# An attention, Fourier-mix and feed-forward kernel: the places of 1750 stage instances in program order, from a formula of offsets to a table

## The chip, the core and the metric

The kernel runs on one core of a Trainium2 chip. Its engines are TensorE (PE, matmul; its weight loads are listed as PEld), VectorE (DVE), ScalarE (ACT), GpSimd (POOL) and SyncE (SP), which here only issues DMAs. Each engine executes its own instructions in the order in which the program lists them, and waits at an instruction until what that needs is there. The metric is device time in microseconds (us) of one execution.

## The reference

Eight batches, 8 heads, 576 positions, head size 64; 4608 rows of 512 in all.

```python
out_d   = sm_attn(q_d, k_d, v_d)            # q, k, v averaged over groups of 4 positions
out_up  = np.repeat(out_d, 4, axis=2)       # "pooled" attention, 144 positions
out_loc = softmax over |i - j| < 4 of 0.125 * q k^T, times v      # "local" attention
x = (out_up + out_loc) as [8, 576, 512]
u = x + real(fft(fft(x, axis=1), axis=2))   # mix
un = (u - mean) / sqrt(var + 1e-6)
return u + relu(un @ w_ch1) @ w_ch2         # 512 -> 2048 -> 512
```

The two weights come as 64-bit floats.

## The kernel before

The work is written as small stages, each a method that issues the instructions of one step, mostly on one engine. Four classes belong to the attention stage.

- `Pooled(b)`, for each batch b, in pairs of heads h0 = 0, 2, 4, 6: `sum_v` (a load on SP and three adding loads on POOL), `scores` (PE), `maxima` (DVE), `exps` (ACT), `transpose_p` (PE), `copy_p` (ACT), `values` (PE), `result` (DVE). It needs `sums`, q and k added up over groups of 4.
- `Unit(b, m)`, five for a batch, for the local attention: `load` and `load_v` (SP), `sum_in` (DVE, makes `sums`), then `scores`, `maxima`, `exps`, `transpose_p`, `copy_p`, `values`, `result` on the same engines as above.
- `Mix(b)`, the two Fourier transforms as matmuls: `half_sum` (DVE) and `half_difference` (POOL) of the results of units, `channels` and `fold` (DVE, half of the folds POOL), `split_high` (ACT) and `split_low` (POOL), `sequence` (PE, four of them, 12 matmuls each) with `sequence_high` (ACT) and `sequence_low` (DVE), a small `sequence_z`, then `mix` (PE), `even_out` (ACT), `unfold` (DVE) and the stores.
- `Quarter(n)`, 64 of them, decodes a quarter of one of 16 weight pairs f to two 32-bit parts: `fetch` (SP), `size` (ACT), `clamp` (POOL), `join` (three DVE instructions), `high` (ACT), `low` (POOL). The first three pairs are decoded during the attention stage, the other 13 only when memory of that stage has come free (`close_a`, `close_e`, `close_d`).

`Block(n)`, nine blocks of 512 rows, is the feed-forward stage: `load` (SP and POOL), `stats` and `norm` (DVE), `turn` (PE transposes, four tiles i), `turn_high` (ACT), `turn_low` (DVE), then for each f `first` (12 matmuls), `high` (ACT), `low` (DVE), `second` (12 matmuls), at the end `finish` (DVE) and `store` (SP). Blocks 0 and 1 run f = 0 to 4 first, then block 0 runs f = 5 to 15, then block 1, then the others.

The program's order comes from one list. Each `plan` method calls `at(t, stage)` with a due time t, and at the end the stages are issued by rising t. The due times are a formula: batch b begins at 20 b plus a small offset, unit u at 4 u, and each kind of stage has one offset that serves all its instances (`AT`, single numbers with two decimals). So all batches have nearly one pattern. Only the order on each engine and queue comes out of it, no wait: waits come from the data and from buffers. There are eight PSUM banks, which `bank` gives out from two pools of four in turn; six buffers for q and k (`NUM_QKT`), three for v (`NUM_V`).

Of the kernel before, what the change touches and what calls it, by code (L numbers as in the profile page):

```python
# [24 lines left out]
PACE = 20  # L25
AT = {

    "pooled": (-1.26, -1.46, -2.33, -2.53, -2.41, -2.33, -2.18, -2.27),
    "local": (0, 0.05, 0, 0, 0, 0, 0.06, 0),
    "mix": (25.89, 25.9, 24.42, 25.07, 25.13, 25.15, 25.13, 25.42),  # L30
    "local_steps": (0, 1.6, 4, 5, 6.17, 8.25, 9.86),
    "pooled_steps": (-0.43, 1.18, 2.76, 3.93, 5.01, 7.14, 8.75),
    "qk": (-10, 1.51),
    "sums": (-3.66, 0.28),
    "sum_v": (-10.41, -9.02, -3.44, 3.04),
    "load_v": (5.42,),
    "store_pooled": (1.92,),
    "pooled_splits": (0.67, 1.6, 0.62, 0.79, 0.69, 1.28, 2.49),
    "halves": (0.22, 1.82, -0.65, 1.49),
    "splits": (0.89, 2.15, 0.3, 0.93, 0.62, 1.76, 2.52),  # L40
    "z": (1.09, 5.07, 6.35, 6.73, 7.92),
    "sequence": (8.13, 2.44, 0.85, 1.44),
    "mixed": (16.42, 1.41, 1.07, 1.26, 2.3, 4.23),
    "tail": (22, 1.18, 1.17, 1.26, 1.53, 2.62),
    "store_local": (2.48,),
    "ffn": (5.82, 1.6),
    "decode": (38.91, 6.9, 4.13, 1.26, 4.33),
    "decode_steps": (-1.51, -0.25, 0.38, 2.01, 2.74),
    "first_norms": (1.77, 1.65, 6.94, 0.87),
    "second_norms": (0.74, 1.38, 3, 1.5),  # L50
    "add": (17.46, 2.35, 4.1),
# [3 lines left out]
CHUNKS = (3, 5, 9, 16)  # L55

ROUND = 5
TILES = 4
# [7 lines left out]
def kernel(  # L66
# [13 lines left out]
    nc = tc.nc  # L80
# [143 lines left out]
    def pooled_at(b):  # L224
        return PACE * b + AT["pooled"][b]

    def pooled_end(b):
        return pooled_at(b) + 15 + AT["pooled_steps"][-1]

    def unit_at(u):  # L230
        return 4 * u + AT["local"][u // NPAIR]

    def mix_at(b):
        return PACE * b + AT["mix"][b]

    events = []

    def at(t, fn, *args):
        events.append((t, len(events), partial(fn, *args)))
# [4 lines left out]
    class Pooled:  # L244
# [97 lines left out]
        def plan(self):  # L342
            b = self.b
            stages = [self.scores, self.maxima, self.exps, self.transpose_p, self.copy_p, self.values, self.result]
            for r in range(4):
                at(pooled_at(b) + AT["sum_v"][r], self.sum_v, r)
            for i in range(H // 2):
                t, h0 = pooled_at(b) + 5 * i, 2 * i
                for d, fn in zip(AT["pooled_steps"], stages):
                    at(t + d, fn, h0)  # L350
# [738 lines left out]
```

## Time and profile before

| | |
|---|---|
| median of three runs | 1195.04 us (1194.35 to 1195.20) |
| the profiled execution, its own time | 1197.92 us |
| span of its trace | 1196.1 us |
| instructions | 20340 |
| PE busy, share of the span | 1126.6 us, 94% |
| DVE busy | 578.1 us, 48% |
| ACT busy | 362.9 us, 30% |
| POOL busy | 304.7 us, 25% |

The profile is of one execution. A share of busy time over the whole span hides the stages: attention and mix lie in the first 370 us, the decoding of weights and the first rounds of the feed-forward stage between 370 and 500 us, the rest of the feed-forward stage behind. Idle time of an engine is put down to what ended it, its releaser.

### The profile page before, as it was taken

How to read it: one execution, taken by the hardware profiler on the slowest of the kernel's cores; microseconds unless marked ns; L12 is line 12 of the kernel's file. 1: busy time of each engine (PE TensorE's matmuls, PEld its weight loads, DVE VectorE, ACT ScalarE, POOL GpSimd, SP SyncE). 2: the span in 40 equal slices, each digit the busy share in tenths (PEclk: the TensorE clock that was granted, in tenths of full speed). 3: DMA queues.
4: the chain of work that ended last, by engine and by line, in shares of the span. 5: the costliest groups of instructions: out<-in, count | busy, mean ns of one | idle time of the engine just before them, and what ended most of it. 6: DMA issues, size and time to landing. Idle time of an engine off the chain costs nothing.

```text
span 1196.1 us, 20340 instructions
## 1 busy us (share of the span) xinstructions
PE 1126.6 (94%) x8172; PEld 950.9 (79%) x8172; DVE 578.1 (48%) x1226; ACT 362.9 (30%) x1050; POOL 304.7 (25%) x411
## 2 busy tenths in 40 slices
PE   4988988989977999999999999999999999999998
PEld 4777977978866888878788888888788888888886
DVE  3798988978888988532222222222222222222111
ACT  3566756757643444211111111111111111111110
POOL 2145536425448556320300200300200300200000
PEclk7888988989988999999999999999999999999999
DMA  8577658569658444250600600600600600600000
GB/s 262 185 209 239 169 168 260 156 198 275 158 120 216 138 129 124 74 111 4 137 1 1 141 1 1 141 1 1 141 1 1 141 1 1 141 1 1 36 1 35
DMA packets 57902, 123.07 MB, mean 103 GB/s; under 512 B 7280, under 2 KB 7408, under 8 KB 57552
## 3 DMA queue, kind: packets, MB, share of 16 engines
q1 hardware_dynamic: 44288, 92.23, 24.1%
q0 software_dynamic: 13520, 29.55, 14.3%
q8 instruction: 64, 1.05, 0.4%
q14 instruction: 30, 0.25, 0.1%
HBM read 89.88 MB, written 30.74 MB: 101 GB/s over the span
## 4 chain that ended last, share of the span: by engine, by line
PE 76%; DVE 11%; DMA 9%; issue 1%; ACT 1%; POOL 1%; SPq 0%; DVEq 0%; POOLq 0%; ACTq 0%
PE hps L814 30%; PE acc L832 10%; PE acc L834 10%; PE acc L833 10%; PE y L578 4%; DMA vsum<-in_vg_dram 2%; DMA ut<-ud 2%; PE av L457 2%; DVE xs L520 2%; DVE w L531 2%; DMA qkT<-in_qk_dram 2%; PE avd L311 2%; PE tpn L785 1%; PE sc L398 1%; DVE o L641 1%
## 5 line engine op out<-in xcount | busy, mean ns | idle before, releaser
L822 DVE SCALAR_TENSOR_TENSOR hl<-hps,hh 128x512 fp32r<-128x512 f32 x144 | 99.4, 690 | 455.4 <-ACT hh L818 455.0
L814 PE MATMUL hps<-unT,w1h 128*128 128x512 f32 x1152 | 311.6, 392 | 1.8 <-ACT even L630 1.2
L814 PEld LDWEIGHTS hps<-unT,w1h 128*128 128x128 f32 x1152 | 215.2, 188 | 47.7 <-ACT even L630 1.4
L818 ACT ACTIVATE hh<-hps 128x512 fp32r<-128x512 f32 x144 | 86.1, 598 | 547.2 <-PE hps L814 547.2
L832 PE MATMUL acc<-w2h,hh 128*128 128x512 f32 x576 | 226.7, 394 | 0.0
L834 PE MATMUL acc<-w2h,hl 128*128 128x512 f32 x576 | 225.3, 391 | 0.0
L833 PE MATMUL acc<-w2l,hh 128*128 128x512 f32 x576 | 225.2, 391 | 0.0
L814 PE MATMUL hps<-unT,w1l 128*128 128x512 f32 x576 | 155.2, 391 | 0.0
L814 PEld LDWEIGHTS hps<-unT,w1l 128*128 128x128 f32 x576 | 108.2, 188 | 23.7
L834 PEld LDWEIGHTS acc<-w2h,hl 128*128 128x128 f32 x576 | 108.2, 188 | 23.6
L832 PEld LDWEIGHTS acc<-w2h,hh 128*128 128x128 f32 x576 | 108.3, 188 | 22.6
L833 PEld LDWEIGHTS acc<-w2l,hh 128*128 128x128 f32 x576 | 108.3, 188 | 22.6
L770 POOL TENSOR_TENSOR rstd<-rstd,mhalf 128x1 f32<-128x1 f32 x36 | 20.7, 575 | 307.5 <-DVE rstd L769 307.5
L755 POOL DMA_DIRECT2D ut<-ux x40 | 35.6, 1058 | 209.6 <-DMA ut<-um 207.4
L416 ACT ACTIVATE sb<-sc,mx 128x64 f32<-128x64 f32 x320 | 69.8, 329 | 1.3
L457 PE MATMUL av<-vaug,pT 64*64 64x65 f32 x1280 | 48.8, 230 | 5.9 <-DMA vaug<-in_vw_dram 5.5
L384 DVE TENSOR_REDUCE sums<-qkT 128x224 f32<-128x896 f32 (+4 forms) x48 | 43.3, 944 | 17.5 <-DMA qkT<-in_qk_dram 16.3
L457 PEld LDWEIGHTS av<-vaug,pT 64*64 64x64 f32 x1280 | 44.7, 145 | 8.4 <-issue 6.1
L398 PEld LDWEIGHTS sc<-qkT 64*64 64x64 f32 x1280 | 48.2, 147 | 3.8 <-issue 1.1
L794 DVE TENSOR_TENSOR unT<-tpn,unT 128x512 fp32r<-128x512 f32 x36 | 24.8, 688 | 53.2 <-ACT unT L791 53.2
L398 PE MATMUL sc<-qkT 64*64 64x64 f32 x1280 | 48.1, 230 | 0.0
L558 POOL TENSOR_TENSOR fl<-xeo,fh 128x512 fp32r<-128x512 f32 x32 | 44.0, 1376 | 15.1 <-ACT fh L555 14.9
(97 smaller groups left out, 1442.8 us busy)
## 6 DMA issues: line engine op xcount, KB each, us to landing
qkT<-in_qk_dram SPq DMA_DIRECT2D x40, 512.0 KB
raw<-in_wq_dram SPq DMA_DIRECT2D x64, 256.0 KB
vaug<-in_vw_dram SPq DMA_DIRECT2D x40, 260.0 KB
out_dram<-ut SPq DMA_DIRECT2D x36, 256.0 KB
um<-o SPq DMA_DIRECT2D x16, 512.0 KB
ut<-ux POOLq DMA_DIRECT2D x32, 256.0 KB, 5.5
ut<-ud POOLq DMA_DIRECT2D x32, 256.0 KB, 5.4
vsum<-in_vg_dram POOLq DMA_DIRECT2D x24, 292.5 KB, 6.4
```

Of the source, the lines that this page charges most:

```text
L384: nc.vector.tensor_reduce(out=to, in_=x[:, :, a - g0 : e - g0], axis=AX.X, op=ALU.add)
L398: nc.tensor.matmul(sc[r, a * W : (a + 1) * W], self.qkT[r, 0, a // 2, o : o + W], self.qkT[r, 1, a // 2, o : o + W], start=False, stop=Tru ...
L416: nc.scalar.activation(out=self.sb[:, a], in_=self.sc[:, a * W : (a + 1) * W], func=AF.Exp, scale=0.125, bias=self.mx[:, a : a + 1],)
L457: nc.tensor.matmul(av[r, a, :], pT[r, 4 * hh + a], va[r, 4 * hh + a, :], start=True, stop=True)
L558: nc.gpsimd.tensor_sub(out=self.fl[:, t], in0=self.x[t], in1=self.fh[:, t].bitcast(F32))
L578: nc.tensor.matmul(y, l, r, start=(i == 0), stop=(i == len(mms) - 1))
L814: nc.tensor.matmul(hps, a[:, c, :], unT[:, x, c, :], start=(i == 0), stop=(i == len(mms) - 1))
L818: nc.scalar.activation(out=hh, in_=self.hps[f], func=AF.Relu)
L822: nc.vector.scalar_tensor_tensor(out=hl, in0=self.hps[f], scalar=0.0, in1=self.hh[f].bitcast(F32), op0=ALU.max, op1=ALU.subtract)
L832: nc.tensor.matmul(acc, hh, w2h, start=start, stop=False)
L833: nc.tensor.matmul(acc, hh, w2l, start=False, stop=False)
L834: nc.tensor.matmul(acc, hl, w2h, start=False, stop=stop)
```

## The change

Every stage instance up to a certain point of the program gets its own place, a whole number from 0 to 1749, in a table with one row for each kind of stage (`TURNS`). `at` takes the next number of the row of its stage; an instance for which the row has run out (the feed-forward stage from block 1, f = 9, on) keeps a due time by the old formula and comes behind all places. All 2502 stage instances are there before and after, and each issues the same instructions. Two small edits go along: `sums`, `yh`, `o` and `ends` are allocated by whichever of their stages comes first, since that is no longer always the same one.

```diff
-PACE = 20
-AT = {
...
-    "pooled_steps": (-0.43, 1.18, 2.76, 3.93, 5.01, 7.14, 8.75),
-    "qk": (-10, 1.51),
-    "sums": (-3.66, 0.28),
-    "load_v": (5.42,),
-    "local_steps": (0, 1.6, 4, 5, 6.17, 8.25, 9.86),
-    "halves": (0.22, 1.82, -0.65, 1.49),
-    "sequence": (8.13, 2.44, 0.85, 1.44),
-    "first_norms": (1.77, 1.65, 6.94, 0.87),
...
+ITEM = 1.6
+TURNS = {
...
+    "Unit.load": (
+        0, 2, 1, 6, 8, 44, 43, 42, 72, 73, 104, 154, 153, 150, 157, 155, 288, 294, 292, 357, 361, 358, 402, 405,
+        476, 530, 528, 657, 656, 658, 751, 752, 814, 820, 816, 879, 881, 947, 946, 981,
+    ),
...
+    "Unit.load_v": (
+        9, 5, 4, 45, 102, 106, 152, 149, 158, 232, 230, 289, 355, 362, 360, 406, 471, 472, 475, 529, 560, 653,
+        655, 698, 695, 753, 818, 817, 822, 880, 943, 945, 944, 984, 1032, 1098, 1099, 1097, 1163, 1161,
+    ),
...
+    "Unit.scores": (
+        17, 16, 34, 38, 40, 57, 108, 122, 111, 146, 220, 251, 282, 256, 341, 320, 387, 386, 469, 500, 524, 591,
+        601, 623, 707, 708, 720, 759, 760, 857, 810, 908, 926, 968, 973, 1013, 1061, 1109, 1087, 1111,
+    ),
...
+    "Unit.maxima": (
+        20, 22, 49, 60, 61, 87, 115, 138, 139, 203, 239, 265, 301, 295, 391, 334, 436, 443, 488, 538, 558, 607,
+        633, 681, 714, 716, 766, 778, 779, 865, 853, 934, 940, 977, 980, 1042, 1072, 1120, 1107, 1132,
+    ),
...
+    "Mix.sequence_low": (
+        229, 217, 238, 243, 376, 407, 414, 411, 557, 556, 559, 573, 711, 733, 693, 712, 892, 897, 891, 893,
+        1023, 1041, 1022, 1058, 1175, 1201, 1176, 1192, 1296, 1297, 1275, 1273,
+    ),
...
+    "Block.stats": (1159, 1154, 1178, 1157, 1323, 1295, 1324, 1351, 1747),
...
+    "Block.norm": (1202, 1203, 1231, 1217, 1331, 1303, 1379, 1380),
...
+    "Block.turn": (1208, 1209, 1232, 1219, 1335, 1375, 1407, 1406),
...
+    "Block.turn_low": (1216, 1233, 1260, 1276, 1349, 1402, 1416, 1421),
...
+    places = {name: iter(turns) for name, turns in TURNS.items()}
     events = []
...
-    def at(t, fn, *args):
-        events.append((t, len(events), partial(fn, *args)))
+    def at(fn, *args, t=0.0):
+        owner = getattr(fn, "__self__", None)
+        name = fn.__name__ if owner is None else f"{type(owner).__name__}.{fn.__name__}"
+        place = next(places.get(name, iter(())), None)
+        events.append((place is None, t if place is None else place, len(events), partial(fn, *args)))
...
-            t = unit_at(self.u)
-            for fn, (first, step) in ((self.load, AT["qk"]), (self.sum_in, AT["sums"])):
-                at(pooled_at(self.b) + first + step * self.m, fn)
-            at(t + AT["load_v"][0], self.load_v)
-            stages = [self.scores, self.maxima, self.exps, self.transpose_p, self.copy_p, self.values, self.result]
-            for d, fn in zip(AT["local_steps"], stages):
-                at(t + d, fn)
+            for fn in (
+                *(self.load, self.sum_in, self.load_v, self.scores, self.maxima, self.exps),
+                *(self.transpose_p, self.copy_p, self.values, self.result),
+            ):
+                at(fn)
...
-        for _, _n, fn in sorted(events, key=lambda e: e[:2]):
+        for *_, fn in sorted(events, key=lambda e: e[:3]):
```

Sorting the stages by the formula and by the table gives the order on each engine. Of the 2502 instances 756 keep their place in the whole list; the first that moves is the first of all, the last is number 2390. Some stretches of the two orders (P is Pooled, U is Unit; arguments are batch and unit or head):

```
PE, its first 15 stages
formula: P.scores(0,0) U.scores(0,0) P.transpose_p(0,0) P.scores(0,2) U.scores(0,1) U.transpose_p(0,0) P.values(0,0)
         P.transpose_p(0,2) U.scores(0,2) U.values(0,0) P.scores(0,4) U.transpose_p(0,1) P.values(0,2) U.scores(0,3) ...
table:   U.scores(0,1) U.scores(0,0) P.scores(0,0) P.scores(0,2) U.transpose_p(0,0) P.transpose_p(0,0) U.values(0,0)
         U.scores(0,2) P.scores(0,4) U.transpose_p(0,1) P.transpose_p(0,2) U.scores(0,3) P.scores(0,6) U.scores(0,4) P.values(0,0)
SP, its first loads
formula: P.sum_v(0,0) U.load(0,0) (0,1) (0,2) (0,3) (0,4) U.load_v(0,0) P.sum_v(1,0) U.load(1,0) U.load_v(0,1) U.load(1,1) ...
table:   U.load(0,0) (0,2) (0,1) P.sum_v(0,0) U.load_v(0,2) (0,1) U.load(0,3) (0,4) U.load_v(0,0) U.load(1,2) (1,1) (1,0) ...
DVE, from the last result of a unit on
formula: result(7,4) channels(7,2,0) channels(7,2,1) stats(0,1) fold(7,2,0) unfold(6,1,0) half_sum(7,1) unfold(6,1,1)
         channels(7,1,0) stats(0,2) channels(7,1,1) fold(7,1,0) half_sum(7,0) stats(0,3) norm(0,0) ... turn_low(0,3)
table:   result(7,4) fold(7,3,0) half_sum(7,0) sequence_low(6,3) sequence_low(6,1) norm(0,0) ... turn_low(0,3)
PE, from the last values of a unit on
formula: values(7,4) mix(6,1,0) mix(6,1,1) turn(0,0) sequence_z(7) turn(0,1) turn(0,2) sequence(7,0) turn(0,3) first(0,0)
         sequence(7,1) first(0,1) sequence(7,2) second(0,0)
table:   values(7,4) sequence(6,3) sequence(6,1) mix(6,0,0) turn(0,0) turn(0,1) mix(6,1,1) sequence_z(7) turn(0,3) mix(6,0,1)
         turn(0,2) sequence(7,3) (7,2) (7,1) (7,0) first(0,0) first(0,1) second(0,0)
```

Counts on the two orders: PE stages between a unit's `scores` and its `transpose_p`, 8.8 on average by the formula and 13.3 by the table; DVE stages between a unit's `maxima` and its `result`, 18.4 and 22.6; DVE stages between a batch's last `fold` and its first `sequence_low`, batches 0 to 7, 10, 10, 9, 9, 7, 8, 5, 9 and 11, 7, 14, 11, 19, 13, 15, 8; PE stages between a pooled `transpose_p` and its `values`, 4.2 and 3.7; DVE stages between the last result that a `half_sum` needs and that `half_sum`, 12.9 and 6.8; the loads of q and k stand 29 places earlier in the whole list, on average. Of the 580 calls of `bank`, 9 by the formula and 125 by the table come at a point of the list at which all four banks of the pool that is due are held by stages whose last reader is listed later.

## Rows read from the trace of the kernel before

**Rows 1.** The head of the page: the span; PE's busy time in 40 slices of 30 us, in tenths; DVE's.

```profile
span 1196.1 us, 20340 instructions
...
PE   4988988989977999999999999999999999999998
...
DVE  3798988978888988532222222222222222222111
```

**Rows 2.** Busy time by stretch (windows): stretch and its length, busy us (instructions) of PE, PEld, DVE, ACT and POOL, granted clock, mean busy share of the DMA engines, GB/s.

```profile
0.00:20.00 20.00, 9.05 (x102) 7.91 (x104) 7.46 (x12) 3.69 (x11) 4.70 (x14) 0.74 0.85 254
20.00:50.00 30.00, 23.30 (x386) 20.13 (x384) 17.50 (x45) 17.93 (x71) 5.39 (x10) 0.81 0.80 250
50.00:100.00 50.00, 45.08 (x693) 40.04 (x690) 41.80 (x101) 31.97 (x116) 19.68 (x25) 0.91 0.60 167
100.00:150.00 50.00, 45.47 (x673) 40.62 (x671) 46.66 (x108) 33.57 (x118) 27.29 (x31) 0.90 0.72 219
150.00:200.00 50.00, 43.64 (x587) 39.45 (x587) 41.08 (x96) 28.16 (x99) 21.04 (x27) 0.86 0.66 192
200.00:250.00 50.00, 46.40 (x695) 41.84 (x696) 47.39 (x119) 35.38 (x124) 26.34 (x34) 0.97 0.74 225
250.00:300.00 50.00, 42.87 (x652) 38.83 (x650) 38.45 (x92) 31.49 (x112) 18.38 (x23) 0.93 0.75 218
300.00:350.00 50.00, 47.84 (x703) 44.42 (x704) 40.40 (x106) 31.01 (x109) 20.10 (x27) 0.97 0.58 138
350.00:400.00 50.00, 34.12 (x188) 29.56 (x187) 45.29 (x92) 18.28 (x44) 37.36 (x47) 0.83 0.73 180
400.00:450.00 50.00, 48.85 (x223) 39.98 (x222) 45.65 (x92) 22.08 (x54) 27.30 (x45) 1.00 0.47 132
450.00:500.00 50.00, 50.00 (x222) 41.46 (x221) 39.83 (x74) 20.40 (x50) 27.80 (x43) 1.00 0.35 100
...
600.00:700.00 100.00, 100.00 (x449) 82.32 (x448) 24.30 (x44) 12.90 (x22) 9.23 (x12) 1.00 0.19 42
```

**Rows 3.** The waits of PE over the whole span: engine, line that waited, releaser, total us, times, longest.

```profile
PE tpn L785 <- DVE un L777: 16.5, 4, 14.8
...
PE sp L266 <- DVE sums L384: 11.6, 2, 9.9
...
PE avd L311 <- DMA vsum<-in_vg_dram: 4.9, 1, 4.9
...
PE mix L623 <- DVE o L641: 3.9, 1, 3.9
```

**Rows 4.** The waits of DVE between 15 and 370 us, same columns.

```profile
DVE yl L588 <- ACT yh L585: 11.8, 9, 3.3
...
DVE mx L411 <- PE sc L398: 8.7, 9, 2.5
...
DVE sums L384 <- DMA qkT<-in_qk_dram: 8.0, 3, 4.0
...
DVE rsd L322 <- PE avd L311: 7.9, 3, 7.2
```

**Rows 5.** From the timeline of the first 62 us, three engines' queues (start, length, engine, line, operation, tiles, count, idle before): first PE's, then SP's loads of q and k for batch 1, then the DVE that sums them up.

```profile
15.09 1.24 PE L266 MATMUL sp<-sums 64*72 64x144 f32 x8 [9.94 <-DVE sums L384]
...
26.78 2.15 PE L311 MATMUL avd<-vsum,ptd 72*72 72x65 f32 x16 [4.88 <-DMA vsum<-in_vg_dram]
...
18.57 13.94 SPq L366 DMA_DIRECT2D qkT<-in_qk_dram  x3
...
41.33 4.11 DVE L384 TENSOR_REDUCE sums<-qkT 128x224 f32<-128x896 f32 x5
```

**Rows 6.** The transposes of block 0 and its first matmuls, from the timeline between 345 and 375 us, same columns.

```profile
365.44 1.09 PE L785 MATMUL tpn<-ident,un 128*128 128x128 f32 x4 [14.79 <-DVE un L777]
...
373.46 1.20 PE L814 MATMUL hps<-unT,w1h 128*128 128x512 f32 x4 [0.67 <-ACT unT L791]
```

**Rows 7.** A piece of the chain that ended last, between 380 and 390 us: start, us, what; one `sequence` and one `first`.

```profile
385.34 1.60 PE y L578 x12
...
386.94 2.82 PE hps L814 x12
```

**Rows 8.** VectorE between 352 and 366 us, from the timeline: the last instructions of `result(7,4)`, two `half_sum` (L520) and the first `norm` (L777).

```profile
353.43 0.75 DVE L475 TENSOR_TENSOR xb<-av,rs 128x256 f32<-128x256 f32 x2
...
357.18 3.31 DVE L520 TENSOR_TENSOR xs<-xa,xb 128x512 f32<-128x512 f32 x1
...
363.14 0.69 DVE L520 TENSOR_TENSOR xs<-xa,xb 128x512 f32<-128x512 f32 x1
...
364.75 0.54 DVE L777 TENSOR_SCALAR un<-ut,mv,rstd 128x512 f32<-128x512 f32 x1
```

**Rows 9.** Groups of instructions by line and form: engine, operation, tiles, shapes, count, busy us, mean ns, idle before. `half_sum`, then `channels` of the sums and of the differences.

```profile
L520 DVE TENSOR_TENSOR xs<-xa,xb 128x512 f32<-128x512 f32 x24 | 26.0, 1082 | 0.0
...
L531 DVE TENSOR_TENSOR w<-xs 128x255 f32<-128x255 f32 x24 | 17.4, 727 | 0.1
...
L531 DVE TENSOR_TENSOR w<-xm 128x255 f32<-128x255 f32 x24 | 10.4, 433 | 0.0
```

**Rows 10.** The last weight of a `first`: GpSimd's low part of pair 15, and that pair's first use on PE, from the timeline between 484 and 505 us.

```profile
492.16 0.74 POOL L191 TENSOR_TENSOR w1l<-wt,w1h 128x256 fp32r<-128x256 f32 x1 [1.76 <-ACT w1h L187]
...
493.71 1.07 PE L814 MATMUL hps<-unT,w1h 128*128 128x512 f32 x4
```

More of the change, by code (lines that the diff above doesn't have):

```diff
@@ L372, in sum_in @@
         def sum_in(self):
-            if self.m == 0:
+            if self.b not in sums:
                 sums[self.b] = pd.tile([P, 2, HP, G], F32, name="sums", bufs=1)
@@ L649, in store_mixed @@
             k0 = TAIL * (self.b % 2)
-            for half, o in enumerate(self.o):
+            for half in range(2):
                 dst = um[self.b][half, k0 : k0 + 2 * P, :].rearrange("(t k) c -> k t c", t=2)
-                nc.sync.dma_start(out=dst, in_=self.o[o])
+                nc.sync.dma_start(out=dst, in_=self.o[half])
         def store_ends(self):
@@ L675, in plan @@
         def plan(self):
-            t = mix_at(self.b)
-            local = list(reversed(range(NSL)))
-            first, step, first_m, step_m = AT["halves"]
-            for i, slot in enumerate(local):
-                at(t + first + step * i, self.half_sum, slot)
-                at(t + first_m + step_m * i, self.half_difference, slot)
-            for begin, name, these in ((pooled_end(self.b), "pooled_splits", [NSL]), (t, "splits", local)):
-                first, step, odd, minus, plus, high, low = AT[name]
-                for i, slot in enumerate(these):
-                    u = begin + first + step * i
-                    at(u, self.channels, slot, 0)
-                    at(u + odd, self.channels, slot, 1)
-                    at(u + minus, self.fold, slot, 1)
-                    at(u + plus, self.fold, slot, 0)
-                    at(u + high, self.split_high, slot)
-                    at(u + low, self.split_low, slot)
@@ L721, in plan @@
-            at(unit_at(NPAIR * self.b + NPAIR - 1) + AT["local_steps"][-1] + AT["store_local"][0], self.store_local)
+            for slot in reversed(range(NSL)):
+                at(self.half_sum, slot)
+                at(self.half_difference, slot)
+            for slot in reversed(range(NSL + 1)):
+                for odd in range(2):
+                    at(self.channels, slot, odd)
+                for minus in range(2):
+                    at(self.fold, slot, minus)
+                at(self.split_high, slot)
+                at(self.split_low, slot)
@@ new lines, in plan @@
+            for pooled in (True, False):
+                at(self.split_z, pooled)
+            for fn in (self.sequence_z, self.z_high, self.z_low):
+                at(fn)
+            for T in range(4):
+                for fn in (self.sequence, self.sequence_high, self.sequence_low):
+                    at(fn, T)
+            for slot in range(2 + self.b % 2):
+                at(self.mix, slot, 0)
+                at(self.even_out, slot)
+                at(self.mix, slot, 1)
+                for minus in range(2):
+                    at(self.unfold, slot, minus)
@@ L867 @@
         u.plan()
[L868 to L880 removed]
+    at(constants)
+    at(clear_yz)
     def close_b():
```

308 lines of the change are left out of this document (187 added, 121 removed), and 32 rows, old and new, of the table TURNS.

## The prediction

> **What bounds the kernel now.** I read the head of the page first, then busy time by stretch, then the waits of PE and of DVE, then the timelines of the start and of the handover to the feed-forward stage. The slices [rows 1] show three regimes. From some 500 us on PE is at 9 tenths or more and DVE at 2 or 3: PE does 100 of 100 us at full clock [rows 2], and no order of stages can shorten that. Between 40 and 500 us DVE is as full as PE. From 50 to 350 us the six rows of DVE add up to 255.8 of 300 us and those of PE to 271.3, so DVE stands 44.2 us and PE 28.7 us [rows 2]. Before 50 us both are short of data: DVE does 25.0 of 50 us, PE 32.4 [rows 2]. From 350 to 400 us DVE does 45.3 of 50 us and PE only 34.1 [rows 2], most of which is one wait of 14.8 us for the first `norm` [rows 3, 6].
>
> So the end is set like this: a fixed piece of full PE work behind 500 us, and before it a stage in which DVE is nearly the limit, PE waits for DVE at some places and DVE for PE or a load at others. All that a new order can do is to take out idle time before 500 us: of PE some 63 us (the rows to 500 us add up to 436.6 us of PE) and of clock. Where the granted clock of a row is under 1 [rows 2], its PE time is longer by about that share: 0.26 of 9, 0.19 of 23, 0.09 of 45, 0.10 of 45, 0.14 of 44, 0.03 of 46, 0.07 of 43, 0.03 of 48, 0.17 of 34, together some 33 us, an estimate.
>
> **The change, part by part.** It removes and adds no operation; every term is idle time, so each is bounded by the idle time of its stretch. I took the two orders apart by engine; the counts are those given with the change.
>
> *The start, to 50 us.* By the formula PE's first stage is `scores` of the pooled attention, which needs the sums of five loads and starts at 15.1 us after a wait of 9.9 us; the seventh stage then waits 4.9 us for the sum of v [rows 3, 5]. By the table two `scores` of units come first, which need one load each, and the pooled `values` that waited is the fifteenth stage: the eight stages that now stand before it cover 4.9 us with about 1 us each, if v comes no later. Against that, two of the five loads are issued behind a load of the sum of v (292.5 KB) and two of v (260 KB), 0.81 MB or 3.2 us at 254 GB/s [rows 2], so the pooled stages begin up to 3 us later. Batch 1's loads stand 13.9 us in SP's queue until `scores` of units free their buffers, and DVE sums them only at 41.3 us [rows 5]; the table has those `scores` earlier. Between nothing (the loads run at 0.80 and more of the DMA engines all the while [rows 2]) and -10 us (9.9, or 4.9 and as much for batch 1) I take -5, the wait of 4.9 us that has an evident cover.
>
> *50 to 350 us.* DVE's named waits up to 370 us are 11.8 us of `sequence_low` for PE and ScalarE, 8.7 of `maxima` for `scores`, 8.0 of the sums for loads, 7.9 of a pooled `result`, 7.2 of these at once in the start [rows 4]. The table pulls producers forward and pushes consumers back: between the last `fold` and the first `sequence_low` of a batch lie 12 DVE stages on average instead of 8, between a unit's `scores` and its `transpose_p` 13.3 PE stages instead of 8.8, and the loads of q and k stand 29 places earlier in the list. What waits is then covered by work of the same engine. If all of 11.8, 8.7 and 8.0 went, it would be -28; but PE and DVE are both over 85% full here, and with one wait gone the next comes soon after. Pooled `values` follow their `transpose_p` closer than before (3.7 stages for 4.2, and in one case none), which costs PE some waits for ScalarE, free as long as DVE is the later one. Ends 0 and -28; I take half, -14.
>
> *The handover.* After the last `result` of a unit DVE has 13 stages before the first `norm`, from 354.2 us to 364.8 us, 10.6 us of which one `half_sum` takes 3.3 [rows 8]; by the table four stages. Three of the `stats` and other work of the thirteen now stand ahead of that `result`, so not all of 10.6 us is won. PE gets two `sequence` (1.6 us each [rows 7]) into the gap that was empty. Against it, all four `sequence` of batch 7, 6.4 us, now stand before the first `first`, which was behind one of them; this is work that had to be done anyway, not a loss, but the last `turn_low` is also three stages later in DVE's order. Ends 0 and -14.8 (the gap [rows 6]); I take half, -7.
>
> *The clock.* 33 us of PE time are due to the lower level, and it falls where PE has stood: 0.83 in the stretch with the gap of 14.8 us against 1.00 behind it [rows 2, 6]. A third less idle time should give some of it back: 0 to -8, taken -3.
>
> *The first rounds of the feed-forward stage.* In four cases (f = 0 and 15 of block 0, f = 1 of block 1, f = 7 of block 0) only one `first` of 2.8 us [rows 7] stands between `first` and its own `second`, where there were two stages. One ScalarE and one VectorE instruction must fit under it, behind whatever DVE has queued (45.7 of 50 us busy [rows 2]). Never shown before; bounds nothing and +5 (one wait of PE for DVE is 3.9 us [rows 3], for one case of four and a little for the others); taken +2.
>
> Sum: -5 - 14 - 7 - 3 + 2 = -27. The profiled execution's span is 1196.1 us, its own time 1197.9, 2.9 above the median of 1195.0; the difference applies to both, so I predict 1195 - 27 = 1168 us. If every term took half of its amount, 1182; with all terms nearer to their ends, -45, 1150.
>
> **What could eat some of it.** `half_sum` took 0.69 us in one place and 3.31 in another, where a GpSimd instruction ran beside it, 1.08 on average; `channels` of the sums 0.73, of the differences 0.43 [rows 8, 9]. Undisturbed the 24 and 24 would take 16.6 and 10.4 us instead of 26.0 and 17.4, so 16.4 us of DVE go that way. By the table a `half_sum` comes 6.8 stages after the result that frees it, not 12.9, and GpSimd's `half_difference` waits for the same result: they meet more often. If the loss doubled, +16, the sum would be -11, 1184 us; this lies in the forecast's own range. The Trainium skill (SBUF — State Buffer, Who interferes with whom) states that a VectorE instruction with two SBUF inputs contends with a GpSimd instruction that reads SBUF and that the order of issue decides which of them blocks; by that rule such a meeting costs either engine, and the stretched rows agree.
>
> **The rivals.** *The banks (slower).* The table makes PE run far ahead: 125 calls for a PSUM bank against 9 come when the list still holds all four. Where this happened before, a matmul of `mix` stood 3.9 us until an `unfold` had read its bank [rows 3]. PE has 28.7 us to lose from 50 to 350 us [rows 2]; 116 more calls use that up at 0.25 us each. At 0.35 us they cost 40.6 us, 12 more than PE has, and start and handover give nothing as the whole stage is late: 1207 us. Against it: the list's place says little of time where DVE, which frees the banks, is not held up itself, and then a full set of banks only means that DVE always has work waiting.
>
> *The weights (no change).* GpSimd finishes the last weights of pair 15 at 492.9 us and PE uses them at 493.7, 0.8 us later [rows 10]. Should the decoding end when it did, any gain before it is lost again there, and the time stays within 0.2%, 1195 us. For it: DVE, which does most of the decoding, is 91% busy from 400 to 450 us [rows 2]. Against it: the decoding starts with memory that the attention stage frees, in the table's order as in the formula's after about the same DVE work, so it moves along with the handover; and from 450 to 500 us DVE has 10.2 us to spare [rows 2].
>
> **How the numbers follow.** Forecast 1168, own range 1150 to 1184, 79%; weights 1195, 7%; banks 1207, 14%. About 0.2% or 2.4 us is what a measurement of this kernel tells from no change. Faster 0.79, same 0.07, slower 0.14. The range of 8 in 10 has to take in the own range, its tail above 1184 and the weights: 1150 to 1198, which leaves out most of the banks and what lies under 1150.
>
> **What would show it.** Start: PE's first stage well before 15 us and no wait for the sum of v. Middle: DVE's six rows of 50 us fuller, the waits of `sequence_low`, `maxima` and sums under half of 28 us. Handover: the gap of 14.8 us before the first transposes under 8 us. Clock: rows nearer to 1. Feed-forward: PE without gaps of over 1 us between the first `first` and 500 us, and the last weights still just in time, but some 25 us earlier. I am wrong if PE stands for banks (releasers `unfold`, `result`, `exps` before matmuls that don't read them), if DVE's busy time before the handover grows, or if the last weights come at 493 us again.

## The result, and the profile after

The changed kernel took 1150.51 us (median of 4 runs, 1145.82 to 1151.62) against 1194.69 (4 runs): ratio 0.962, 95% interval 0.959 to 0.965, 44.2 us less. The forecast was 1168, 27 less. The direction was right and the size too small: the time lies at the low edge of the range of 1150 to 1198 (by the ratio, 0.9622 of 1195.04 us, it is 1149.9). Idle time fell where the prediction looked for it; what PE loses at its lower clock was put far too low. The profiled execution after is the fastest of its four (1145.82 us, span 1144.0) and that of before was 2.9 us above its median, so the two profiles differ by 52 us, 8 more than the medians.

The head of the page after: span, busy time of the engines, then PE's and DVE's busy slices and the granted clock, in slices of 28.6 us; it answers [rows 1].

```profile
span 1144.0 us, 20389 instructions
...
PE 1108.0 (97%) x8172; PEld 935.8 (82%) x8172; DVE 545.4 (48%) x1226; ACT 358.4 (31%) x1050; POOL 293.5 (26%) x411
...
PE   7899999899889999999999999999999999999998
...
DVE  4889999899878776322212222222222222222111
...
PEclk7999999999999999999999999999999999999999
```

PE (with its weight loads), DVE, ACT and POOL have as many instructions as before; the 49 more of the total are not theirs. PE executes the same 8172 matmuls in 1108.0 us instead of 1126.6, 18.6 us less. The record of the clock in the traces says where from: before, 60.4 us of PE's work lie in stretches at half clock, after, 20.2 us, which is 30 and 10 us more than at full clock. In slices the clock is at 9 (90% or more) in all but the first. A second profile of the same order (t_all, below) has PE at 1110.5 us, 16.1 less than before. PE's idle time, span less busy time, is 36 us instead of 69.5. Idle and clock together are the 52 us.

Busy time by stretch after, columns as in [rows 2].

```profile
0.00:20.00 20.00, 13.14 (x142) 11.18 (x144) 8.44 (x14) 5.20 (x18) 4.70 (x14) 0.68 0.87 286
20.00:50.00 30.00, 26.45 (x508) 23.42 (x505) 22.51 (x62) 21.92 (x89) 9.16 (x14) 0.93 0.87 253
50.00:100.00 50.00, 45.99 (x774) 41.31 (x774) 43.66 (x119) 36.87 (x135) 27.98 (x35) 1.00 0.86 254
100.00:150.00 50.00, 47.64 (x715) 43.18 (x714) 47.91 (x118) 36.35 (x128) 24.12 (x31) 1.00 0.73 221
150.00:200.00 50.00, 48.13 (x737) 43.53 (x735) 46.74 (x126) 35.85 (x127) 25.00 (x32) 1.00 0.81 251
200.00:250.00 50.00, 45.49 (x720) 40.92 (x719) 44.78 (x107) 33.86 (x123) 22.46 (x29) 0.97 0.73 206
250.00:300.00 50.00, 49.13 (x778) 46.10 (x779) 45.84 (x129) 37.53 (x133) 26.71 (x35) 1.00 0.78 207
300.00:350.00 50.00, 42.49 (x297) 37.04 (x296) 39.75 (x97) 20.67 (x48) 34.54 (x48) 0.97 0.73 185
350.00:400.00 50.00, 49.82 (x229) 40.44 (x228) 40.68 (x86) 21.06 (x53) 23.32 (x41) 1.00 0.41 128
400.00:450.00 50.00, 50.00 (x221) 41.21 (x220) 37.88 (x78) 20.38 (x52) 25.15 (x43) 1.00 0.34 104
```

Against [rows 2] PE does more matmuls in each row to 300 us, and four of the five rows from 50 to 300 us are at full clock, where they were at 0.86 to 0.93: from 150 to 200 us PE is busy for 48.1 us at 1.00 where it was for 43.6 at 0.86. The clock is no higher in the first 20 us (0.68 for 0.74) and from 200 to 250 us (0.97 in both). The six rows of DVE from 50 to 350 us add up to 268.7 us for 255.8. From 300 us on the rows hold other work than before, since the feed-forward stage begins earlier.

The same columns with cuts at the end of the last `result` of batch 0 and of batch 7, which bound nearly the same work in both; first the kernel before, then after.

```profile
0.00:60.45 60.45, 41.63 (x630) 35.99 (x630) 31.20 (x76) 27.70 (x102) 13.23 (x28) 0.80 0.73 223
60.45:354.19 293.74, 262.67 (x3847) 237.68 (x3847) 253.60 (x607) 186.09 (x653) 133.88 (x164) 0.92 0.68 196
354.19:1196.00 841.81, 822.33 (x3695) 677.21 (x3695) 293.28 (x545) 149.07 (x296) 157.60 (x221) 0.99 0.26 62
```

```profile
0.00:49.23 49.23, 39.59 (x644) 34.60 (x645) 30.18 (x74) 26.35 (x102) 13.08 (x27) 0.83 0.87 265
49.23:306.14 256.91, 241.89 (x3799) 219.88 (x3799) 235.43 (x616) 182.80 (x649) 131.71 (x168) 0.99 0.78 226
306.14:1144.00 837.86, 826.48 (x3731) 681.35 (x3729) 279.79 (x540) 149.24 (x301) 148.67 (x217) 1.00 0.25 62
```

Length less PE's busy time is PE's idle time: 18.8, 31.1, 19.5 before, 9.6, 15.0, 11.4 after. So 36.8 of the 52 us come out of the middle, and more than half of that (20.8) is PE's busy time, most of it clock: the middle's matmuls are nearly as many (3799 for 3847), the granted clock 0.99 for 0.92.

The waits of PE after (the longest, whole span), columns as in [rows 3], then DVE's between 10 and 340 us, as in [rows 4].

```profile
PE y L744 <- ACT fh L721: 3.8, 1, 3.8
...
PE avd L483 <- DMA vsum<-in_vg_dram: 3.2, 3, 1.2
PE tpn L932 <- DVE un L924: 2.9, 3, 1.4
PE sc L559 <- ACT sb L584: 2.4, 3, 1.7
PE sp L438 <- DVE sums L552: 2.3, 1, 2.3
...
PE mix L789 <- ACT sb L584: 1.5, 1, 1.5
```

```profile
DVE rs L639 <- PE av L625: 8.3, 15, 2.1
DVE unT L941 <- ACT unT L938: 5.8, 3, 4.3
DVE sums L552 <- DMA qkT<-in_qk_dram: 4.7, 5, 2.2
...
DVE rsd L494 <- PE avd L483: 2.2, 4, 1.0
...
DVE yl L754 <- ACT yh L751: 1.6, 2, 1.2
```

No wait of PE is over 4 us; before, there were waits of 14.8, 9.9 and 4.9. DVE's waits for `sequence_low` fell from 11.8 to 1.6 and those for the sums from 8.0 to 4.7; the wait of a unit's `result` for its `values` has grown from 1.9 us in 7 pieces to 8.3 us in 15, the mark of a VectorE that is ahead of PE.

The handover after, from PE's timeline, columns as in [rows 6], then the last low part of pair 15 on GpSimd and that pair's first weight load of this part and first matmul, as in [rows 10].

```profile
310.32 1.11 PE L932 MATMUL tpn<-ident,un 128*128 128x128 f32 x8 [1.09 <-DVE un L924]
...
321.67 1.82 PE L744 MATMUL y<-seqm,fh 128*128 128x290 f32 x6 [3.77 <-ACT fh L721]
...
329.32 1.10 PE L958 MATMUL hps<-unT,w1h 128*128 128x512 f32 x4
...
446.11 0.74 POOL L371 TENSOR_TENSOR w1l<-wt,w1h 128x256 fp32r<-128x256 f32 x1
...
446.84 1.07 PE L958 MATMUL hps<-unT,w1h 128*128 128x512 f32 x4
447.52 0.87 PEld L958 LDWEIGHTS hps<-unT,w1l 128*128 128x128 f32 x4
```

The gap of 14.8 us is one of 1.1, with 3.8 later for the last split. The first `first` comes 44 us earlier than before, and so do the weights: the last one lands at 446.85 and is loaded at 447.5.

### The profile page after: what moved, and what is told of

It reads as the page before. It is cut to its first block, busy times and chain, and to the rows that moved or that the text cites. A ratio compares the mean times of both kernels' runs of the same rounds, so it can differ in the third digit from the quotient of the medians.

```text
span 1144.0 us, 20389 instructions
## 1 busy us (share of the span) xinstructions
PE 1108.0 (97%) x8172; PEld 935.8 (82%) x8172; DVE 545.4 (48%) x1226; ACT 358.4 (31%) x1050; POOL 293.5 (26%) x411
## 4 chain that ended last, share of the span: by engine, by line
PE 79%; DVE 10%; DMA 6%; issue 2%; SPq 1%; ACT 1%; POOL 0%; DVEq 0%; ACTq 0%; POOLq 0%
PE hps L958 34%; PE acc L976 11%; PE acc L978 11%; PE acc L977 11%; DMA vsum<-in_vg_dram 3%; PE y L744 2%; PE av L625 1%; PE avd L483 1%; PE sc L566 1%; PE tpn L932 1%; DVE sums L552 1%; DMA raw<-in_wq_dram 1%; PE mix L789 1%; DVE xeo L710 1%; DVE w L697 1%
## 5 line engine op out<-in xcount | busy, mean ns | idle before, releaser
L958 PEld LDWEIGHTS hps<-unT,w1l 128*128 128x128 f32 x576 | 108.3, 188 | 23.6
L902 POOL DMA_DIRECT2D ut<-ux x40 | 35.5, 1002 | 206.7 <-DMA ut<-um 206.3
L625 PEld LDWEIGHTS av<-vaug,pT 64*64 64x64 f32 x1280 | 42.2, 138 | 6.3 <-issue 2.9
```

Of the source, the lines that this page charges most:

```text
L625: nc.tensor.matmul(av[r, a, :], pT[r, 4 * hh + a], va[r, 4 * hh + a, :], start=True, stop=True)
L902: nc.gpsimd.dma_start(out=to, in_=ux[b][k0 : k0 + m, :], accum_op=ALU.add)
L958: nc.tensor.matmul(hps, a[:, c, :], unT[:, x, c, :], start=(i == 0), stop=(i == len(mms) - 1))
```

## The experiments

b_fill and the four kernels named for an engine (b_dve, a_dve, b_pe, a_pe) add work, a_warm adds warm-up; all others issue the same instructions and change only the numbers in the table. Costs are ratios to the kernel before on the same chip, with their 95% interval, turned into us of its 1192 to 1194.

**Parts of the change in time.** A table in which the first places come from one order and the rest from the other, here one row of it:

```diff
 "Unit.scores": (          # changed kernel
-    17, 16, 34, 38, 40, 57, 108, 122, 111, 146, 220, 251, 282, 256, 341, 320, 387, 386, 469, 500,
 "Unit.scores": (          # h_start: table for 110 places, then formula
+    17, 16, 34, 38, 40, 57, 108, 137, 169, 200, 221, 254, 291, 327, 362, 384, 418, 457, 498, 529,
...
 "Mix.sequence_low": (     # h_att: table for 1100 places, then formula; its last eight
-    1023, 1041, 1022, 1058, 1175, 1201, 1176, 1192, 1296, 1297, 1275, 1273,
+    1023, 1041, 1022, 1058, 1140, 1151, 1160, 1172, 1262, 1283, 1299, 1324,
```

> The first 110 places of the list follow the table, all others the formula. Theory A (the gain is PE's idle time, taken out stretch by stretch, and with it the low clock that stood behind each of those waits): the start alone is worth what the changed kernel won there, 7.2 us of PE's idle time before 50 us, and some of the low clock at 25 and 46 us comes back, so 1183 to 1188 us against 1194.7. Rival C (the gains are one chain, the start gives nothing while DVE's order behind it is the old one, because DVE catches up later at its own pace): within 2.5 us of the kernel before, and the idle time taken out before 50 us shows again as waits between 50 and 350 us.

Measured: 0.9969 (0.9945 to 0.9993), 3.7 us less, near the prediction's 5, though under theory A's 7 to 12. The interval, 0.8 to 6.6 us, does not rule out rival C's 2.5 here.

> The first 1100 places follow the table (start and attention up to the last batch), the rest the formula, so that the handover to the feed-forward stage keeps its old order. Theory A: start (7.2), middle (15) and the greater part of the low clock (some 12 of 18.6 us of PE's busy time) are won, the handover's 9.3 us and the low clock behind it are not: 1158 to 1164 us. Rival C (the handover decides): over 1180 us, with the time won earlier lost again in the wait for the first norm, which would then be well over 14.8 us.

Measured: 1162.9 us, 0.974 (0.970 to 0.977), 31.5 less: theory A. Its handover still has the old wait:

```profile
PE tpn L1008 <- DVE un L1000: 14.8, 1, 14.8
```

> The first 1100 places follow the formula, the rest the table: the handover alone. Theory A: the gap of 14.8 us shrinks to under 5 us and the 17 us at half clock behind it go as well, some 8 us of PE's time: 1176 to 1184 us. Rival C (the handover decides): 1165 us or less. If the two halves are additive, the gain here and the gain of the kernel that has only the attention part by the table add up to 44 us within 4 us.

Measured: 0.9958 (0.9939 to 0.9977), 5.0 less, under theory A's 11 to 19 and far from rival C. PE's timeline in its handover:

```profile
353.01 1.11 PE L1008 MATMUL tpn<-ident,un 128*128 128x128 f32 x8 [1.09 <-DVE un L1000]
...
364.23 1.82 PE L820 MATMUL y<-seqm,fh 128*128 128x290 f32 x6 [3.61 <-ACT fh L797]
```

The gap is gone as in the changed kernel, 14.8 against 1.1, and 3.6 of it come back at the split; the first `first` comes at 371.95 us, only 1.5 us earlier than in [rows 6]. Theory A also counted 17 us at half clock behind the gap as 8 us of PE's time. The trace of the kernel before has only 4.1 us of PE's work in that stretch, most of which lies in the gap itself, so 2 us at most were to be had. The stretches are worth 3.7 (start), 31.5 - 3.7 = 27.8 (middle) and 5.0 alone or 12.7 (44.2 - 31.5) behind a reordered middle; the two differences are good to some 5 us. Rival C, one place that decides all, is out. The two halves add up to 36.5 of 44.2 us, not within the 4 us that were expected of additive parts: the handover seems to be worth more behind the new middle.

**The clock by itself.** The old order, and matmuls without use in seven waits of PE:

```diff
+FILL = {(1, 0): 13, (2, 6): 18, (4, 0): 13, (7, 0): 19}
...
+            two = [bank("sp", GH) for _ in range(2)]
+            fill(two[0], FILL.get((self.b, h0), 0))
...
+            fill(tp, 120 if (self.n, i) == (0, 0) else 0)
```

> The order of before, unchanged; seven of PE's waits (at 45, 60, 73, 109, 154, 258 and 365 us) are filled with matmuls without use, of the two transposes' unit matrix, into the bank that the stage behind the wait overwrites. They are 13 to 120 in number, each of some 0.1 us, about as long as the wait was. PE waits for the same data as before, but it has not stood. Theory A (the low clock is a price of its own, paid behind each wait): the low periods behind these seven waits go (6.83, 3.41, 3.41, 10.24, 6.83, 6.83 and 17.07 us, 54.6 us at half clock, up to 27 us of PE's time); where DVE is not late anyway this shows in the time: 8 to 15 us faster than before, 1180 to 1187 us. Rival B (the low clock only goes along, DVE sets the time there): the granted clock is 1 and the time stays within 2.5 us of before, or is some us longer where the filling outlasts the wait.

Measured: 1.0038 (1.0018 to 1.0058), 4.5 us *longer*. The filling of the handover's wait and its stretch, in the timeline and in the windows:

```profile
353.19 13.28 PE L247 MATMUL tpn<-ident 128*128 128x256 bf16 x120
368.07 0.66 PE L796 MATMUL tpn<-ident,un 128*128 128x128 f32 x4 [1.60 <-DVE un L787]
```

```profile
350.00:400.00 50.00, 46.38 (x335) 39.88 (x335) 45.41 (x89) 17.83 (x42) 38.15 (x48) 1.00 0.77 188
```

The filling ends 1.6 us before the first `norm` is there, and the clock of the stretch is 1.00 where it was 0.83 [rows 2]. From this transpose to the first matmul of `first` with pair 15 the trace has 128.1 us, before 128.3 [rows 6, 10]: a full clock behind the greatest wait was worth 0.2 us. But little was at stake there: the 17 us at half clock hold 4.1 us of PE's work, 2 us more than at full clock. Over the whole span PE is busy for 1147.9 us, of which the 249 matmuls without use take 33.8 (by lines), so PE's own work took some 1114 us instead of 1126.6, 12 us faster, and none of it shows in the time. In five of the other six places the next stage begins as soon as the filling ends, so that there it may have outlasted the wait; that part of the 4.5 us is not separated. The mean granted clock is 0.979 for 0.964, not 1 as rival B had it. So theory A's 8 to 15 us are refuted for this filling, and rival B is the nearer one; that the low clock costs the old order nothing is not shown.

**Which engine sets the pace.** The same extra work in both orders:

```diff
             nc.vector.tensor_reduce(out=mx, in_=scv, axis=AX.X, op=ALU.max, negate=True)
+            nc.vector.tensor_reduce(out=mx, in_=scv, axis=AX.X, op=ALU.max, negate=True)
```
```diff
+            for _ in range(7):
+                nc.tensor.matmul(sc[:, : 2 * P], one[:, :P], one, start=True, stop=True)
```

> The order of before. The maxima of each unit are computed twice into the same tile: 40 VectorE instructions more, by the 0.68 us of the one that is there, 27 us. Filling PE's waits has shown that the low clock behind them is worth nothing by itself in this order. Theory D (before the handover VectorE sets the pace of the old order, PE's waits and its clock only go along): 18 to 27 us longer than before. Rival P (PE sets the pace in both orders): at most 8 us. Rival L (neither; a chain of waits that changes between them): 9 to 17 us.

> The order of the table, with the same 40 VectorE instructions more (27 us). Against the changed kernel's 1150.5 us: Theory D (the table has filled VectorE's idle time and PE has become the pace): at most 14 us, less than the same work costs in the old order. Rival P: at most 8 us, as in the old order. Rival L: 9 to 17 us, as in the old order. Should it cost the full 27 us, VectorE is still the bound in the new order.

> The order of before, with seven matmuls without use (each some 0.1 us) ahead of each unit's scores, into the bank that these overwrite: 280 more, 30 us of PE's time at full clock. Theory D (VectorE sets the pace of the old order): at most 10 us longer than before. Rival P (PE does): 25 us or more. Rival L: 11 to 20 us.

> The order of the table, with the same 280 matmuls more (30 us). Against the changed kernel's 1150.5 us: Theory D (PE has become the pace): 20 us or more, and clearly more than in the old order. Rival P: 25 us or more, as in the old order. Rival L: 11 to 20 us, as in the old order.

| extra work | in the old order | in the table's order, less the changed kernel's 0.9622 |
|---|---|---|
| VectorE, 27 us | 1.0081 (1.0049 to 1.0114): 9.7 us | 0.9723 (0.9694 to 0.9752): 12 us |
| PE, 30 us | 1.0058 (1.0033 to 1.0083): 6.9 us | 0.9770 (0.9736 to 0.9803): 17.7 us |

(Less 0.9634, the table's order measured again below, the last column is 10.6 and 16.2 us.) No theory holds whole. VectorE is not the pace of the old order: two thirds of 27 us vanish in idle time, as theory L has it. But the 280 matmuls cost more than twice as much in the new order as in the old, as theory D has it, though not in full. Part of that is the clock. PE's busy time is 1126.6 us in the old order and 1108.0 in the new without these matmuls; with them the pages of b_pe and then of a_pe have:

```profile
PE 1144.2 (95%) x8452; PEld 962.6 (80%) x8452; DVE 577.5 (48%) x1226; ACT 362.7 (30%) x1050; POOL 303.5 (25%) x411
```

```profile
PE 1139.1 (98%) x8452; PEld 957.6 (82%) x8452; DVE 544.8 (47%) x1226; ACT 358.0 (31%) x1050; POOL 291.4 (25%) x411
```

These are 17.6 and 31.1 us more. In the old order the added matmuls also filled waits, and PE's work at half clock fell from 60 to 28 us; in the new order there was little of it to take back (20 to 15 us). Per us of PE's busy time the cost is 0.4 in the old order and 0.6 in the new, so the difference between the orders is smaller than the table makes it look. In the old order no single engine is the limit; the time goes in waits of one for the other.

**Loads or computing stages.**

```diff
 "Unit.load": (     # f_loads: formula's order, loads moved forward
-    1, 3, 4, 5, 6, 38, 47, 51, 58, 65, 133, 147, 160, 170, 183, 284, 302, 315, 328, 340,
+    0, 2, 1, 6, 8, 44, 43, 42, 68, 73, 104, 150, 154, 153, 172, 200, 288, 292, 296, 354,
...
 "Unit.load": (     # t_loads: table's order, loads where the formula has them
-    0, 2, 1, 6, 8, 44, 43, 42, 72, 73, 104, 154, 153, 150, 157, 155, 288, 294, 292, 357,
+    1, 3, 4, 5, 6, 38, 47, 51, 58, 65, 133, 147, 160, 170, 183, 284, 302, 315, 328, 340,
```

> All stages that compute keep the formula's order; only the loads on SP and POOL move forward, to about the places that the table gives them: those of q and k by 23 places of the list on average (the table: 29; six buffers and the formula's order of the units allow no more), those of v by 16 and the sums of v by 9. Theory W (what the table wins in the middle is mostly data that is there in time): 15 us or more faster than before. Rival O (it is the order of the computing stages, which leaves each engine something to do while another works): within 5 us of before.

> The reverse: all stages that compute follow the table, the loads stand where the formula has them among those stages (29, 16 and 9 places later than the table's). Against the changed kernel's 1150.5 us: Theory W: 15 us or more longer, with waits of VectorE for the tiles of q and k and of PE for v. Rival O: at most 6 us longer.

Measured: f_loads 1.0304 (1.0281 to 1.0327), 36 us *longer*; t_loads 0.9649 (0.9626 to 0.9671), 1151.0 us, the gain nearly whole. Rival O. The waits of SP's queue to 400 us and of PE from 50 to 300 us in f_loads:

```profile
SPq L610 <- PE sc L642: 108.3, 14, 15.7
```

```profile
PE av L701 <- DMA vaug<-in_vw_dram: 8.9, 1, 8.9
PE avd L559 <- DMA vsum<-in_vg_dram: 7.1, 1, 7.1
```

A load that is issued early stands in its queue until a buffer is free (108 us in all for `scores`, before 23.6), and the loads of v behind it can stand with it: the two waits of PE for v above are 16 us. What the rest of the 36 us is was not separated. By t_loads the 29 places by which the table has the loads earlier are no part of the gain: without them the time is 0.9649, with them 0.9634 (t_all below), within the intervals.

**The table again, and a warm start.**

```diff
-WARM_UP = 40
+WARM_UP = 80
```

> The order of the table for all 2502 instances, written as places throughout: the same order on every engine as in the changed kernel, to be compared with the others of this call on one chip. Both theories: 0.962 of the time of before, 1147 to 1152 us.

> The changed kernel with 80 matmuls of the warm-up ahead of its first stage in place of 40, so that PE does not stand from 4.8 to 8.3 us, right before its clock falls to half for 17 us; 13.8 us of PE's work lie in these 17 us, 6.9 us more than at full clock. Theory D (in the new order PE sets the pace, so the clock counts): 3 to 7 us faster than the same order with 40. Rival (at the start the loads set the pace, PE's clock counts for nothing there): within 2 us of it, with the same work done by 50 us.

Measured: t_all 0.9634 (0.9606 to 0.9662), 1149.5 us; a_warm 0.9668 (0.9634 to 0.9701), 1154.9, not faster. The start of a_warm, PE's timeline:

```profile
9.63 1.10 PE L566 MATMUL sc<-qkT 64*64 64x64 f32 x32
15.10 2.20 PE L438 MATMUL sp<-sums 64*72 64x144 f32 x16 [4.37 <-DVE sums L552]
```

The first two `scores` of units run at full clock, and PE then waits 4.4 us for the sums instead of 2.3: the loads set this place, the clock has nothing to give. The rival's "same work done by 50 us" does not hold in this profile: PE has done 104 matmuls fewer by then, warm-up apart, behind a wait of 5.0 us for the sum of v (3.2 in t_all, 1.2 in the changed kernel's profile).

**Classes of stages, and mean shifts.** Each stage wanted its place of one order or the other, or a mean; pairs that stand the same way round in both orders kept it.

```diff
 "Mix.sequence_low": (
-    197, 212, 224, 244, 359, 374, 387, 409, 516, 535, 547, 562, 681, 697, 708, 727, 846, 862,   # formula
+    225, 216, 233, 245, 370, 396, 402, 399, 551, 549, 552, 566, 703, 725, 699, 716, 885, 890,   # x_mix
+    214, 212, 226, 240, 377, 393, 398, 412, 535, 548, 555, 571, 691, 706, 707, 725, 862, 890,   # x_nomix
+    219, 221, 227, 240, 375, 397, 398, 405, 549, 556, 558, 567, 704, 724, 709, 726, 876, 887,   # t_mean
```

> The stages of the Fourier mix follow the table, all others the formula, as far as pairs of stages that stand the same way round in both orders allow: on VectorE 580 of the 1283 pairs that the table turns round are turned, on PE 185 of 655. Theory M (the win comes from the mix: half sums right behind the result that frees them, sequence_low later behind its sequence): 25 us or more faster than before. Rival S (the parts don't add, each stage needs the others' new places around it): within 8 us of before.

> The complement: the attention, load, decoding and feed-forward stages follow the table, the mix follows the formula, within the same bounds: 641 of the 1283 pairs on VectorE are turned, 428 of 655 on PE. Theory M: within 10 us of before. A rival that has the attention stages carry the gain (scores further ahead of their transposes, maxima further ahead of the results): 25 us or more faster. Rival S: within 8 us of before, and the sum of this gain and that of the kernel with only the mix by the table is far under 44.

> Every attention and mix stage stands at its place by the formula plus the mean shift that the table gives its kind (and its number within the batch) over the eight batches, kept to pairs that stand the same way round in both orders; the rest as in the table. So all batches have the new leads and nearly one pattern again: on VectorE 759 of 1283 pairs are turned, on PE 378 of 655. Theory K (the leads of the kinds are the gain, a formula with other offsets would have done): 30 us or more faster than before. Rival I (the single places count, each fitted to where its neighbours stand): less than 20 us faster.

Measured: 1.0195 (1.0163 to 1.0227), 1.0324 (1.0297 to 1.0352) and 1.0250 (1.0218 to 1.0282): 23, 39 and 30 us *longer* than before. No theory had expected a loss; of what is on record only rival I's "less than 20 us faster" covers it. The blends are not between the two orders in time, they are worse than both; these mean leads with the formula's regularity did not do it. Other offsets were not tried.

**A little disorder.**

```diff
 "Unit.scores": (
-    17, 16, 34, 38, 40, 57, 108, 122, 111, 146, 220, 251, 282, 256, 341, 320, 387, 386,   # changed kernel
+    16, 17, 33, 40, 42, 60, 106, 124, 111, 149, 222, 252, 286, 258, 345, 324, 387, 391,   # j_table
```

> The table, with up to 8 places added or taken at random for each computing stage among the first 1740, kept to pairs that stand the same way round in both orders: 123 pairs turned on PE, 229 on VectorE, a mean shift of 1.6 places. Theory I (the gain lies in the single places): 20 us or more longer than the changed kernel's 1150.5 us. Rival G (the table's gross order carries it, only blends with the formula break it): at most 8 us longer.

> The formula's order disturbed in the same way (up to 16 places, kept to the same pairs, which leaves it 118 turned pairs on PE and 183 on VectorE, a mean shift of 2.7 places). Theory I, if the formula's offsets were as closely fitted: 20 us or more longer than before. If only the table is fitted to its places and the formula is loose: at most 8 us longer. Rival G: at most 8 us.

Measured: j_table 1212.1 us, 1.0159 (1.0132 to 1.0187), 61.6 above the changed kernel; j_formula 1.0249 (1.0230 to 1.0269), 30 above before. Theory I, for both orders and by more than the 20 us that it asked. j_table from 50 to 300 us, in windows and in DVE's waits:

```profile
50.00:300.00 250.00, 221.73 (x3144) 196.38 (x3145) 204.98 (x506) 153.05 (x544) 106.77 (x135) 0.91 0.70 201
```

```profile
DVE rs L715 <- PE av L701: 11.3, 16, 3.5
DVE mx L655 <- PE sc L642: 6.8, 4, 2.8
DVE rsd L570 <- PE avd L559: 5.8, 3, 2.7
```

The waits come back on both sides, and the clock with them, 0.91 for 0.99. The same stretch of ten kernels tells how far each had come (matmuls and VectorE's busy time in 250 us):

| | matmuls done | DVE busy, us | granted clock | time against before |
|---|---|---|---|---|
| before | 3292 | 215.4 | 0.91 | |
| after | 3714 | 228.9 | 0.99 | -44 |
| t_loads | 3731 | 231.7 | 0.99 | -42 |
| h_att | 3639 | 224.5 | 0.97 | -31 |
| j_table | 3144 | 205.0 | 0.91 | +19 |
| x_mix | 3055 | 203.9 | 0.90 | +23 |
| t_mean | 2989 | 206.3 | 0.90 | +30 |
| j_formula | 3049 | 205.9 | 0.90 | +30 |
| f_loads | 2955 | 199.0 | 0.90 | +36 |
| x_nomix | 2926 | 196.4 | 0.90 | +39 |

## Why the prediction was right in direction and too small

**The start** (-5): measured alone 3.7 less, right in size. PE's first stage comes at 8.3 us. The wait for the sum of v, on whose cover the term rested, is 1.2 us instead of 4.9 in the changed kernel's profile, but 2.7 in h_start's, 3.2 in t_all's and 5.0 in a_warm's: the cover holds only in part, and more came from the first stages, which wait 3.5 + 2.3 us for the mask's load and the sums where they waited 11.6. So there is some luck in the 5.

**50 to 350 us** (-14): as PE's idle time right, 16.1 us in the profiles. As an account of the middle it was too small: 36.8 us of length in the profiles, 27.8 by the runs (h_att less h_start). The reason given for it, that waits get covered by work of the same engine, holds for DVE's (`sequence_low` 11.8 to 1.6, sums 8.0 to 4.7), except that the loads' places had no part in it (t_loads).

**The handover** (-7): 5.0 alone, 12.7 behind the reordered middle; the gap went as said, and 3.8 us came back at the split of batch 7. Right within its ends.

**The clock** (-3): this is the step that failed, the term that was mis-sized most. PE's busy time fell by 18.6 us at 8172 matmuls (16.1 in t_all's profile), six times the term and twice its far end of 8. The estimate of 33 us at the lower level was sound (30 us by the record of the clock). What was wrong is the sentence "A third less idle time should give some of it back", and the wait that it looked at. All twelve stretches at half clock before begin during or right behind a wait of PE, and not only behind the gap of 14.8 us but behind waits of 0.7 to 4.5 us as well; after, three are left. The stretch at the gap holds 4.1 of the 60.4 us of PE's work, the nine behind the waits of up to 4.5 us hold 47.9. These small waits went, and nearly the whole middle came to full clock. Even a third of 33 would have been 11. By stretch the same miss is the middle's: 14 us were taken, 27.8 came by the runs. That the time still lies at the edge of the range is luck: its -45 was put together from waits nearer to their ends, with at most 8 us of clock.

The term is no price of the clock alone: in b_fill PE's own work was 12 us faster and the old order gained nothing, though the filling may have cost some of it. Idle and clock are taken here as two views of one loss, PE standing for other engines and then going slower; that is an argument, which the runs support and do not prove. The account of 52 us is right as a sum, not as two causes. In hindsight a better-sized middle can be had from [rows 2] alone: 28.7 us of idle time and, by the shares of the clock in its six rows, some 20 us more. Half of that, the share that the prediction took of DVE's waits, is some 25 us in place of 14 and of the clock term; the sum would have been -5 - 25 - 7 + 2 = -35, or 1160, and the middle near the measured 27.8. The rest of the miss is the handover, worth 5.0 alone and 12.7 behind the new middle.

**The feed-forward rounds** (+2): nothing; PE is busy for 49.8 and 50.0 us of 50 from 350 and from 400 us on.

**What could eat some of it** had the wrong sign. The 24 `half_sum` and 24 `channels` of the sums, by line and form after, against [rows 9]:

```profile
L686 DVE TENSOR_TENSOR xs<-xa,xb 128x512 f32<-128x512 f32 x24 | 18.6, 775 | 0.1
...
L697 DVE TENSOR_TENSOR w<-xs 128x255 f32<-128x255 f32 x24 | 9.9, 414 | 0.1
```

They take 28.5 us instead of 43.4; by these times they meet GpSimd less often, not more. The rule of the Trainium skill (SBUF — State Buffer, Who interferes with whom), that the order of issue decides which of the two is blocked, cannot say the sign from an order of stages; the runs show 0.72 us (t_loads) to 1.58 us (f_loads) on average for one and the same `half_sum`. A faster DVE does not make the gain by itself: in j_table `half_sum` takes 0.76 us and DVE's busy time is 562.2 us, 16 less than before, and the kernel is 19 us slower. But a part of the 44 us may be due to it: DVE's busy time fell by 32.7 us in all, which at the price of b_dve and a_dve (9.7 and 12 us of time for 27 us of DVE) would be 12 to 15 us, an estimate. No run separates this from the order itself.

**The rivals.** *Banks*: matmuls that wait for a reader of their bank lost 2.4 + 1.5 us in the two largest groups and under 8 us in all, not 40; a full set of banks in the list says nothing of time, as the argument against it had it. *Weights*: the decoding moved along, 446.85 us for 492.9.

Left open: why just these places fit. The runs show that the gain does not outlast a small disorder (j_table) or these mean shifts (t_mean), and that no class of stages and no load carries it; that it lies in waits between engines is what the profiles say. Each disorder was drawn once, so how much another draw would cost is not known, and no rule is found by which the table could be drawn up. Changing one engine's order alone, the others' kept, was not tried. None of these kernels is clearly faster than the changed one.

## What to carry to other kernels

Where several engines are 85 to 95% full and wait for each other, count PE's idle time *and* the time that it loses at its low clock behind the waits, taken together; here, pricing the named waits gave half of the middle's gain. Such an order could not be taken class by class or in the mean: moving the stages of either by some two places cost 30 to 60 us, so blends, early loads and fills have to be measured as whole orders. And a wait that was filled (b_fill) or a clock that was raised at the start (a_warm) gained nothing here, where the next stage still waited for another engine or a load.

## What was not expected of the hardware

The granted clock goes with the order: at half for 85 us in the old one, 24 and 31 us in two profiles of the table's, 82 in the disturbed table, at the same matmuls. The same VectorE instruction took 0.72 to 1.58 us on average, by the order alone. Loads issued some 23 places earlier (those of q and k; those of v 16) made the kernel 36 us slower.
